# Attention and a mixture of experts on one core: weight copies and K/V loads in two requests, and another sum for the weights' power of two

## The chip, the core and the metric

The kernel runs on one NeuronCore of a Trainium2 chip. Five engines work side by side, each through its own instructions in order: TensorE (PE, matmuls; PEld is its weight load), VectorE (DVE), ScalarE (ACT), GpSimd (POOL) and SyncE (SP), which here asks for most of the transfers. They wait for each other by semaphores. The metric is the device time of one execution in microseconds; lower is better. The program moves data by 16 DMA engines; SP's requests stand in one queue.

## The reference

Four batches of 12288 queries attend to pooled keys; each row of the result goes through one of 8 experts.

```python
kv_pool = kv.reshape(B, H // r, r, W // r, r, C).mean(axis=(2, 4))    # r = 4: 768 keys per batch
k = v = kv_pool.reshape(B, -1, C) @ w_sr                              # C = 128
a = softmax(q @ k.T / sqrt(C));  x = a @ v                            # 4 x 12288 rows
expert = argmax(normalised x . normalised expert_emb / tau)           # 8 experts, gate = its probability
out[rows of e] = gate * (relu(x @ w1[e]) @ w2[e])                     # w1: 128 x 1024, w2: 1024 x 128
```

## The kernel before

Float32 factors are split into two float16 parts, hi and lo, and a product is three matmuls (hi hi, hi lo, lo hi) where that pays. So that no part over- or underflows, a tensor is first divided by a power of two near its largest entry.

The attention runs in 96 steps of 512 queries (`step_ops`), 24 to a batch. A step forms scores in blocks of 128 queries by 768 keys (`s_mm`), takes the row maximum on DVE (`s_max`; from step 16 on `s_leave`, which also moves the scores out of PSUM), the exponential on ACT (`s_exp`), the hi and lo parts (`p_hi`, `p_lo`), turns them by DMA transposes that SP asks for (`p_t`: tiles `pthi`, `ptlo`) and multiplies by V (`av`: `xp`). Until step 16 three PSUM banks of scores take turns, so a score block must wait until the exponential of three blocks before has read its bank. Rows are scattered to DRAM by expert (POOL), and tiles of 256 rows of one expert come back (`load`) and go through `l1` (x times W1), `h_hi` and `h_lo` (the relu's parts, ACT and DVE), `l2` and `l2_lo` (times W2), and a scatter to the output. Attention steps and expert tiles run at the same time from about 220 us on; the expert tiles alone make up the end.

In the first 180 us `w_ops` prepares the experts' weights: loads W1 and W2 (`wf`), takes the largest entry per partition (`w_max`, or a norm by ACT), finds the power of two over all partitions (`pow2_ops`), makes hi and lo parts (`w_hi`, `w_lo`) and stores them in DRAM as rows of `w_prep`. The order in `pow2_ops`, one link after another: a TensorE transpose of the partitions' maxima into `w_m` (line 441), four DVE instructions on `w_t` (maximum, floor, exponent mask, a diagonal: lines 641 to 653), a matmul with ones that spreads the result to all partitions (line 658), a multiply and a reciprocal on DVE (664, 668). K and V use the same function and keep it.

An expert tile `t` needs its expert's row block of `w_prep` in one of three buffers `wbuf` (`load_w`, 1 MB). The request is conditional: where the buffer already holds that expert, the copy is skipped, but SP still works through the request. K and V source rows of the next batch are loaded ahead in 8 pieces (`kv_load`, 768 KB each, line 453), and summed on DVE or POOL (`kv_adds`, line 467).

No order is written by hand. `Plan` collects operations with an engine, a duration, a key (a due time) and the operations they need, plays them through, and records them in the order in which each engine takes them; ready operations go by their key. A table `X` of numbers sets keys and choices of engine. So a change of a duration, a key or a part moves instructions on all engines, far behind its own place. SP's queue is planned with a number for each transfer's length (`dma=`).

Of the kernel before, what the change touches and what calls it, by code (L numbers as in the profile page):

```python
# [11 lines left out]
F16 = mybir.dt.float16  # L12
# [32 lines left out]
X = dict(  # L45
    ka=16, da=8.159, di=14.892, db=12.933, dma=1.729, ahead=2.284, av=6.502, av0=1.846, lb=-4.518, l2=3.102, qt=1.955,
    lead=18.786, x=-14.465, r=0.691, s=-1.205, p=14.572, x0=3.032, r0=2.092, s0=1.377, p0=5.813, qt0=-0.263,
    pm="acabacbccabcccabbdacccb", pl="aaaaabaa", nm="AAADA", xn="DAAA", nm0="ADD", xn0="AA", we="ddcdcdaaadcdaccd",
    h=13.707, kv=20.916, kvs=2.272, w0=-14.405, start=23.312, early=21.36, wd=12.952, xw=1.718, qd=21, qs=21.178,
    ql=9.747, em="---------AA-A-A-A-AA-DM-", et=2.859, ec=-0.864, v0=123.118, sd=1, qu=1.461, q0=-66.525, avd=0.626,  # L50
    m=1.052, end=-3.563, ne=-4.766, ge=-0.689, kd="DPD", gk=547.052, wq="AADADDAD", kv1=10.617, kvs1=0.757, tg=-0.003,
    tl=0.397, qe="------------------------", gap=1.8, nb="ADDDD-DAAD-A---DDD-A--D-----DDD--A-D-A-D-DA----D",
    sqm="AASAAAAAAAAAPAAAPSSAPPPS", qm="AAADDDADDAADDADAAADAAAAD", xh="ADPPDADPDAADDAAPAADADADD", nl="-",
    slack={'ACT PE': 0.131, 'ACT DVE': 0.095, 'ACT POOL': -0.009, 'ACT ACT': -0.082, 'DVE PE': 0.32, 'DVE ACT': 0.274, 'DVE POOL': 0.348, 'DVE DVE': 0.013, 'PE ACT': 0.263, 'PE DVE': 0.071, 'PE POOL': -0.1, 'PE SP': -0.11, 'POOL ACT': 0.46015762370487345, 'POOL DVE': 0.111, 'POOL PE': 0.1, 'POOL POOL': 0.07},
    wt=4.0, leadr=22.0, wr=55.0, pd=4.0, kf=16, kc="DA", kk=2.199, su=-1.199, vk=-5.844, om="AAAADADA", og=2.027,
)
# [3 lines left out]
def attention_moe(  # L60
# [44 lines left out]
    PTB = 4  # L105
    PB = 3
    Q2 = 3
    NP = 6
    QB = 2
    NQR = 8  # L110
    WC = 4 * F + 8
    WD = 4 * F + 32
    SCALE = 1.0 / math.sqrt(C)
# [60 lines left out]
    scales = cpool.tile([P, 5], F32, name="scales")  # L174
    for i, v in enumerate((1.0 / 4, 1.0 / 8192, 1.0 / 16, math.log(PSC), 0.0)):
        nc.gpsimd.memset(scales[:, i : i + 1], v)
# [25 lines left out]
    wi_i = cpool.tile([P, NTILE], I32, name="wi_i")  # L202
    cpool.tile([P, 72], F32, name="fill")
    ctx.enter_context(tc.manual_schedule())
# [49 lines left out]
    class Plan:  # L254
# [36 lines left out]
        def run(self, begin):  # L291
# [23 lines left out]
            while any(count):  # L315
# [116 lines left out]
    extra = ExitStack()  # L432
    kvs.tile([P, 16], F32, tag="lead", name="lead")
    xp = extra.enter_context(tc.tile_pool(name="early", bufs=1))
# [14 lines left out]
    def kv_load(b, h):  # L449

        t = kvs.tile([P, WD // 2], F32, tag="kvt", name=f"kvt{b}_{h}", bufs=2)
        t = t[:NI, : R * QC].rearrange("p (r c) -> p r c", r=R)
# [743 lines left out]

    def w_scale(e, inv, s):
        ws[e].update(s=s, inv=inv)

    def w_out(e, i):  # L1200

        wo = xp.tile([P, 2 * F + 8 * i], F16, tag=f"wo{i}", name=f"wo{e}_{i}", bufs=1)
        ws[e]["wo", i] = wo
        if i:
            inv = ws[e]["inv"]
            V.tensor_tensor(
                out=wo[:, 2 * F :].bitcast(F32), in0=inv[:, 0:1].broadcast_to([P, 4]),
                in1=inv[:, 1:2].broadcast_to([P, 4]), op=ALU.mult,
            )
# [8 lines left out]
    def w_hi(e, i):  # L1218
        if i == 0:
            w_out(e, 0)  # L1220
        hi = ws[e]["wo", i][:, 0:F]
        if w_eng(e, i) == " AD":
            nc.scalar.mul(hi, ws[e]["w", i], ws[e]["s"][:, i : i + 1])
        else:
            nc.scalar.copy(out=hi, in_=ws[e]["w", i])

    def w_lo(e, i):
        hi, lo = (ws[e]["wo", i][:, h * F : (h + 1) * F] for h in range(2))
# [10 lines left out]
    def w_store(e, i):  # L1239
        nc.sync.dma_start(out=wprep[e * P : (e + 1) * P, 2 * i * F : WC if i else 2 * F], in_=ws[e]["wo", i])  # L1240

# [362 lines left out]
    def weights(t, a, n):  # L1604
        return wbuf[turn_of(t)][:, a : a + n]
# [48 lines left out]
    def l2_terms(t, u, h, parts):  # L1654
# [4 lines left out]
        for i, (kk, j, o) in enumerate(terms):  # L1659
            f = 2 * F + (u * fu + kk) * P + o  # L1660
# [9 lines left out]
    def o_gate(t):  # L1670
        m = ts[t]["m"][:, :, 0:1]
        V.tensor_scalar(out=m, in0=m, scalar1=weights(t, 4 * F, 2).bitcast(F32), scalar2=None, op0=ALU.mult)

    def o_out(t):
        m = ts[t]["m"]
        nj = size(t) // P
        if gated(t):
# [482 lines left out]
    for t in range(NTILE):  # L2160
# [97 lines left out]
```

## Time and profile before

| | us |
|---|---|
| Device time, median of 3 runs (lowest to highest) | 1948.01 (1947.91 to 1948.92) |
| The profiled execution's own time | 1946.91 |
| Its span, first to last instruction | 1945.2 |
| TensorE busy | 1906.0 |
| DVE busy | 1675.1 |
| ACT busy | 1468.7 |
| POOL busy | 1289.4 |

The trace is of one execution, so its times are compared with its own time; the median stands 1.1 us above that. A busy TensorE isn't TensorE at its peak, since its matmuls are pipelined, and small gaps between them aren't seen as idle. [...]

### The profile page before, as it was taken

What the parts mean: (1) busy time and instruction counts of PE and PEld (TensorE: products, weight loads), DVE (VectorE), ACT (ScalarE), POOL (GpSimd) and SP (SyncE); (2) the same over time, 40 slices, a digit from 0 to 9 for tenths busy, and PEclk for the clock granted to TensorE, in tenths of its full rate; (3) what the DMA queues carried; (4) which work ended last, traced back from release to release, by engine and by line L of the source; (5) the groups of instructions that cost most, each with busy time, mean ns of one, the idle gap of its engine ahead of it and who ended that gap; (6) DMA issues with size and microseconds to landing.
All of it is one profiled execution on the core that took longest, in us unless ns stands there. A gap on an engine that the chain in (4) does not pass through costs nothing. (4 is left out here: it accounts for less than half of the span.)

```text
span 1945.2 us, 63642 instructions
## 1 busy us (share of the span) xinstructions
PE 1906.0 (98%) x23536; PEld 1676.3 (86%) x23536; DVE 1675.1 (86%) x4037; ACT 1468.7 (76%) x3162; POOL 1289.4 (66%) x1857
## 2 busy tenths in 40 slices
PE   6999999999999999999999999999999999999998
PEld 5787788888888888888888888888888888889998
DVE  7899999988989879989989988998888888886655
ACT  4887877877787778877778877878878788775553
POOL 2547587678777777676676675756756766666654
PEclk9999999999999999999999999999999999999999
DMA  7998989889988999878989899887878677664353
GB/s 258 250 267 207 205 174 183 165 156 164 170 182 173 190 205 175 172 165 157 193 168 175 180 214 180 171 157 155 176 132 173 149 153 152 148 126 86 107 131 109
DMA packets 870922, 333.23 MB, mean 171 GB/s; under 512 B 825794, under 2 KB 836171, under 8 KB 868432
## 3 DMA queue, kind: packets, MB, share of 16 engines
q1 hardware_dynamic: 844624, 274.95, 71.4%
q0 software_dynamic: 24640, 53.53, 9.7%
q8 instruction: 186, 3.05, 0.7%
q14 instruction: 128, 1.05, 0.2%
q10 hardware_dynamic: 1344, 0.66, 0.1%
HBM read 271.41 MB, written 63.19 MB: 172 GB/s over the span
## 5 line engine op out<-in xcount | busy, mean ns | idle before, releaser
L1632 ACT ACTIVATE hh<-ph 128x512 f16<-128x512 f32 x754 | 447.6, 595 | 224.4 <-PE ph L1625 181.2
L1637 DVE SCALAR_TENSOR_TENSOR hl<-ph,hh 128x512 f16<-128x512 f32 x754 | 513.6, 684 | 109.6 <-ACT hh L1632 103.7
L1625 PE MATMUL ph<-x,wbuf 128*128 128x256 f16 x4416 | 593.2, 273 | 3.2 <-DMA wbuf<-w_prep 2.5
L207 POOL DMA_INDIRECT xs_rows<-rows,pi x384 | 442.0, 1151 | 176.5 <-issue 37.8
L207 POOL DMA_INDIRECT out_dram<-o,m x350 | 382.4, 1093 | 229.0 <-ACT o L1681 45.8
L1625 PEld LDWEIGHTS <-wbuf 128*128 128x128 f16 x4848 | 438.9, 98 | 67.4 <-DMA wbuf<-w_prep 2.9
L1661 PE MATMUL po<-wbuf,hh 128*128 128x128 f16 x6032 | 459.9, 219 | 2.9 <-DVE hl L1637 1.1
L1661 PEld LDWEIGHTS <-hh 128*128 128x128 f16 x6176 | 400.0, 98 | 20.6 <-issue 3.8
L810 PE MATMUL s<-k,qT 128*128 128x512 f16 (+1 forms) x1920 | 364.9, 326 | 1.4 <-DVE nm L821 1.4
L821 DVE CUSTOM_DVE_ANT_0 p<-s,scales,qa 128x768 f32<-128x768 f32 x320 | 323.4, 1011 | 41.6 <-PE s L810 38.9
L875 DVE SCALAR_TENSOR_TENSOR plo<-p,phi 128x768 f16<-128x768 f32 x358 | 350.3, 980 | 5.6 <-ACT phi L861 2.4
L840 ACT ACTIVATE p<-p,nm 128x768 f32<-128x768 f32 x320 | 299.0, 934 | 58.8 <-DVE nm L821 56.8
L926 PE MATMUL xp<-v,pthi 128*128 128x136 f16 (+1 forms) x4392 | 319.7, 223 | 1.4 <-ACT q L738 0.8
L1661 PE MATMUL po<-wbuf,hl 128*128 128x128 f16 x3016 | 291.6, 219 | 0.0
L926 PEld LDWEIGHTS <-pthi 128*128 128x128 f16 x4392 | 278.7, 98 | 14.4 <-issue 2.3
L861 ACT ACTIVATE phi<-p 128x768 f16<-128x768 f32 x310 | 260.9, 844 | 5.9 <-DMA pthi<-phi 2.8
L810 PEld LDWEIGHTS <-qT 128*128 128x128 f16 x1920 | 178.6, 98 | 87.4 <-issue 2.3
L1661 PEld LDWEIGHTS <-hl 128*128 128x128 f16 x3088 | 205.1, 98 | 0.6
L926 PE MATMUL xp<-v,ptlo 128*128 128x136 f16 x2196 | 189.8, 223 | 4.3 <-DMA ptlo<-plo 4.3
L946 ACT ACTIVATE x<-xp,rn 128x135 f32<-128x135 f32 x304 | 96.5, 372 | 76.3 <-DVE rn L938 58.2
L960 POOL TENSOR_TENSOR rows<-x,rows 128x256 f16<-128x256 f32 x192 | 137.2, 719 | 18.2 <-ACT rows L956 13.3
L926 PEld LDWEIGHTS <-ptlo 128*128 128x128 f16 x2196 | 144.0, 98 | 4.8 <-DMA ptlo<-plo 4.8
(416 smaller groups left out, 2043.0 us busy)
## 6 DMA issues: line engine op xcount, KB each, us to landing
wbuf<-w_prep SPq DMA_DIRECT2D x202, 1026.0 KB
q<-in_q_dram SPq DMA_DIRECT2D x48, 512.0 KB
kvt<-in_kv_dram SPq DMA_DIRECT2D x24, 768.0 KB
wf<-in_moe_w_dram SPq DMA_DIRECT2D x16, 512.0 KB
kvt<-in_kv_dram SPq DMA_DIRECT2D x12, 512.0 KB
xs_rows<-rows,pi POOLq DMA_INDIRECT x384
out_dram<-o,m POOLq DMA_INDIRECT x350
w_prep<-wo SPq DMA_DIRECT2D x8, 514.0 KB
```

The lines of the kernel that those rows point to most:

```text
L207: ins = nc.gpsimd.indirect_dma_start(out=dst, out_offset=bass.IndirectOffsetOnAxis(ap=idx, axis=0), in_=src, in_offset=None, bounds_check= ...
L810: nc.tensor.matmul(t[:, lo:hi], qs[:, l, :], r[:, lo:hi], start=i == 0, stop=i == 2)
L821: V.tensor_tensor_reduce(out=p, in0=ks[k].pop(("s", j)), in1=scales[:, 4:5].broadcast_to([P, NK]), scale=ks[k]["fac"], scalar=3.0e38, op0= ...
L840: nc.scalar.activation(out=p, in_=s, func=AF.Exp, bias=ks[k].pop(("nm", j)), scale=1.0 if unscaled(k) else -1.0)
L861: nc.scalar.mul(hi, p, PSC)
L875: V.scalar_tensor_tensor(out=lo, in0=ks[k].pop(("p", j)), scalar=PSC, in1=hi, op0=ALU.mult, op1=ALU.subtract)
L926: nc.tensor.matmul(ks[k]["xp", h][:, i, :e], l[:, c, :], r[:, c, :e], start=n == 0, stop=n == len(terms) - 1, skip_group_check=True,)
L960: nc.gpsimd.tensor_tensor(out=r[:, :, C : 2 * C], in0=ks[k]["x"][:, 2 * h : 2 * h + 2, 0:C], in1=r[:, :, 0:C], op=ALU.subtract)
L1625: nc.tensor.matmul(ph[:, kk * n : (kk + 1) * n], weights(t, o + f, P), r, start=i == 0, stop=i == 2)
L1632: nc.scalar.activation(out=hh, in_=ts[t]["ph", u], func=AF.Relu)
L1637: V.scalar_tensor_tensor(out=hl, in0=ts[t].pop(("ph", u)), scalar=0.0, in1=ts[t]["hh", u], op0=ALU.max, op1=ALU.subtract)
L1661: nc.tensor.matmul(ts[t]["po"][:, j * C : (j + 1) * C], h[:, kk * n + j * P : kk * n + (j + 1) * P], weights(t, f, P), start=u == 0 and i ...
```

## The change

Three parts.

First, weight copies of tiles below 176 and all K/V source loads are asked for in two requests. The first half of a weight copy holds W1 and the scale, which moves from the row's end to its middle and is padded to 32 columns (`WS`); the second half holds W2. `l1` waits for the first, `l2` for the second also. The two halves of a K/V load are two of its four rows each; the sums wait for both. The new function `second` puts the other half on SP's queue at the highest priority, 1.5 us by the plan after the first was taken, so that a request that stands ready in between is taken between them.

Second, the weights' power of two comes from the sum over partitions of the partitions' maxima: one matmul with ones (`total`), a floor and factor in one DVE instruction, the exponent mask and the reciprocal. The factor becomes 1/512 where it was 1/4, since a sum over 128 partitions is up to 128 times the maximum. `sum_ops` takes the place of `pow2_ops` in `w_ops`.

Third, numbers in `X` change: due times and offsets of the first 16 steps, the engines of five weight halves' work (`we`), the engine of the first copy of K for batch 0 (`kc`: from DVE to ACT), and the due times of the weights' work.

```diff
-    pm="acabacbccabcccabbdacccb", pl="aaaaabaa", nm="AAADA", xn="DAAA", nm0="ADD", xn0="AA", we="ddcdcdaaadcdaccd",
+    qt0=0.723, pm="acabacbccabcccabbdacccb", pl="aaaaabaa", nm="AAADA", xn="DAAA", nm0="DDD", xn0="AA",
+    we="ddcccdacddadcccd", h=13.707, kv=20.916, kvs=2.272, w0=-13.574, start=23.312, early=21.36, wd=12.917,
...
-                    if op.dma is not None and u.dma is not None and eng == u.eng and not op.lands:
+                    if op.dma is not None and u.dma is not None and eng == u.eng and not op.lands or u.eng == "~t":
                         ready = op.end
...
+        kv_part(b, h, 0)
+
+    def kv_part(b, h, i):
+        r = slice(i * (R // 2), (i + 1) * (R // 2))
         nc.sync.dma_start(
-            out=t, in_=kv[b].rearrange("(i r) w c -> i r (w c)", r=R)[:, :, h * QC : (h + 1) * QC]
-        )
-        st[b]["kvt", h] = t
+            out=st[b]["kvt", h][:, r, :],
+            in_=kv[b].rearrange("(i r) w c -> i r (w c)", r=R)[:, r, h * QC : (h + 1) * QC],
+        )
...
+    def sum_ops(key, e, room, *deps):
...
+        def total():
+            h["pm"] = one_tile(f"w{e}_m")
+            nc.tensor.matmul(h["pm"][:, 0:2], ones2, ws[e]["m"], start=True, stop=True)
+
+        def scaled():
+            h["inv"] = sm.tile([P, 2], F32, tag="pw2w", name=f"w{e}_2")
+            V.scalar_tensor_tensor(
+                out=h["inv"], in0=h["pm"][:, 0:2], scalar=1e-30, in1=scales[:, 0:2], op0=ALU.max, op1=ALU.mult
+            )
...
+        o = first = add("PE", 0.1, key, total, *deps, take=f"w{e}_m")
+        o = add("DVE", 0.2, key, scaled, o, *room, free=f"w{e}_m")
+        o = add("DVE", 0.17, key, power, o)
+        return first, add("DVE", 0.2, key, inverse, o)
...
-        nc.sync.dma_start(out=wbuf[turn_of(t)][:, :WC], in_=wprep[ds(row, P), :], cond=w < E * P)
+        if t >= NA - PER:
+            nc.sync.dma_start(out=wbuf[turn_of(t)], in_=wprep[ds(row, P), :], cond=w < E * P)
+            return
+        ts[t]["w"] = w, row
+        w_part(t, 0)
+
+    def w_part(t, i):
+        w, row = ts[t]["w"]
+        c = slice(2 * F + WS, WD) if i else slice(0, 2 * F + WS)
+        nc.sync.dma_start(out=wbuf[turn_of(t)][:, c], in_=wprep[ds(row, P), c], cond=w < E * P)
...
+    def second(o, key, fn):
+
+        return add("SP", 0.0, -1e6, fn, add("~t", HALF, key, lambda: None, o))
...
             o = took("kvt", add("SP", 0.45, t0, lambda h=h: kv_load(b, h), *turn("kvt", 2), dma=2.6, hold=True))
+            rest = second(o, t0, lambda h=h: kv_part(b, h, 1))
...
-                r = add(ENG[on], KV_ADD[on][i], t0 + 8.0 + 0.1 * i, fn, o, r, *deps, port=True)
+                r = add(ENG[on], KV_ADD[on][i], t0 + 8.0 + 0.1 * i, fn, o, r, rest, *deps, port=True)
...
-            o, sc = pow2_ops(
-                t0 + 1.2 * d, f"w{e}_", lambda e=e: ws[e]["m"], scales[:, 0:2],
-                lambda inv, s, e=e: w_scale(e, inv, s), scaled.get(e - 2, ()), *m,
-            )
+            o, sc = sum_ops(t0 + 1.2 * d, e, scaled.get(e - 2, ()), *m)
...
+        lw2 = second(lw, kw, lambda t=t: w_part(t, 1)) if t < NA - PER else lw
+        o1, o2, ol = None if whole else o1, lw2, None
```

Two places show how the order moves. The first is TensorE's order near the weights of expert 1, in steps 1 and 2. `s_` are the three score banks, `qT1` and `qT2` the queries of steps 1 and 2, `w1_m` the scale of expert 1; the number at a name's end is the buffer's. Before:

```order
L441 MATMUL w1_m_433<-ident_64,wm1_382 2x128
L803 MATMUL s_1_159<-kf0_255,qT1_314 128x512
L803 MATMUL s_1_159<-kf0_255,qT1_314 128x256
L658 MATMUL w1_m_433<-w1_t_442,ones2_95 128x2
L803 MATMUL s_2_160<-kf0_255,qT2_398 128x512
L803 MATMUL s_2_160<-kf0_255,qT2_398 128x256
L441 MATMUL pq3_483<-ident_64,q2_312 128x128 x4
L803 MATMUL s_0_158<-kf0_255,qT2_398 128x512
L803 MATMUL s_0_158<-kf0_255,qT2_398 128x256
```

The same stretch of TensorE's order now:

```order
L837 MATMUL s_1_159<-kf0_255,qT1_312 128x512
L837 MATMUL s_1_159<-kf0_255,qT1_312 128x256
L443 MATMUL pq3_437<-ident_64,q2_316 128x128 x4
L837 MATMUL s_2_160<-kf0_255,qT2_418 128x512
L837 MATMUL s_2_160<-kf0_255,qT2_418 128x256
L695 MATMUL w1_m_477<-wm1_405,ones2_95 128x2
L837 MATMUL s_0_158<-kf0_255,qT2_418 128x512
L837 MATMUL s_0_158<-kf0_255,qT2_418 128x256
```

The two `w1_m` matmuls around the last block of step 1 have become one, which stands behind the first block of step 2, and `pq3`, the turn of step 3's queries, has moved ahead of that block.

The second place is SP's queue where the weights of tile 98 (`wbuf2`) are asked for. `ptlo63_1` is a part of step 63's second half, `x_101` and `m101` are the rows of tile 101, `kvt3_6` is a K/V load; the quiet rows load and check registers. Before:

```order
L904 DMA_TRANSPOSE pthi63_1_25327<-phi63_1_25070 128x12x128
L904 DMA_TRANSPOSE ptlo63_1_25373<-plo63_1_25292 128x12x128
L1554 TENSOR_LOAD off_i_132
L1554 ISA x2
L1592 ISA
L1592 DMA_TRANSPOSE x_101_25422<-xs_rows 128x2x256
L1593 ISA
L1593 DMA m101_25421<-xs_rows 128x2x2
L1554 TENSOR_LOAD wi_i_133
L1554 ISA x2
L1568 ISA
L1568 DMA wbuf2_2878<-w_prep 128x4104
```

SP's queue at the same place now:

```order
L459 DMA kvt3_6_25340<-in_kv_dram 96x2x512
L938 DMA_TRANSPOSE pthi63_1_25472<-phi63_1_25117 128x12x128
L1585 TENSOR_LOAD wi_i_133
L1585 ISA x2
L1608 ISA
L1608 DMA wbuf2_2885<-w_prep 128x2080
L938 DMA_TRANSPOSE ptlo63_1_25535<-plo63_1_25196 128x12x128
L1608 ISA
L1608 DMA wbuf2_2885<-w_prep 128x2048
```

The copy for tile 98 was asked for behind `ptlo63_1` and the loads of tile 101; its first half now stands ahead of `ptlo63_1`, its second half behind it, and the second half of a K/V load stands ahead of `pthi63_1`.

## Rows read from the trace of the kernel before

**Rows 1.** The page, busy us (share of the span) and instructions of each engine.
```profile
PE 1906.0 (98%) x23536; PEld 1676.3 (86%) x23536; DVE 1675.1 (86%) x4037; ACT 1468.7 (76%) x3162; POOL 1289.4 (66%) x1857
```
**Rows 2.** TensorE's waits, whole span: who waited for whom, total, times, longest.
```profile
PE xp L926 <- DMA ptlo<-plo: 4.3, 2, 2.3
PE w_m L658 <- DVE w_t L653: 3.7, 1, 3.7
PE ph L1625 <- DMA wbuf<-w_prep: 2.5, 2, 2.1
...
PE w_m L441 <- DVE rn L937: 0.9, 1, 0.9
...
PE w_m L658 <- DVE rn L937: 0.5, 1, 0.5
```
**Rows 3.** Timeline of TensorE from 45 us: start, us, operation, idle before and releaser.
```profile
45.43 0.58 PE L658 MATMUL w_m<-w_t,ones 2*128 2x2 f32 x2 [3.67 <-DVE w_t L653]
45.94 2.93 PE L803 MATMUL s<-kf,qT 128*128 128x512 f32 x4
...
49.21 1.46 PE L803 MATMUL s<-kf,qT 128*128 128x512 f32 x4
```
**Rows 4.** Windows: length; PE, PEld, DVE, ACT, POOL busy; PEclk; DMA share; GB/s.
```profile
40.00:45.00 5.00, 1.59 (x5) 0.68 (x4) 5.00 (x11) 5.00 (x7) 1.77 (x1) 1.00 0.53 119
...
46.00:47.00 1.00, 1.00 (x3) 0.48 (x3) 0.97 (x4) 1.00 (x2) 1.00 (x1) 0.50 1.73 166
...
712.00:716.00 4.00, 4.00 (x46) 3.31 (x45) 2.72 (x8) 3.52 (x10) 2.17 (x4) 1.00 0.67 158
...
1165.00:1170.00 5.00, 5.00 (x45) 3.71 (x43) 2.28 (x4) 2.36 (x4) 2.53 (x4) 0.66 0.75 133
```
**Rows 5.** Timeline of DVE, first and fourth link of expert 1's scale.
```profile
41.25 0.27 DVE L641 TENSOR_REDUCE w_t<-w_m 2x1 f32<-2x128 f32 x1
...
43.89 1.48 DVE L653 TENSOR_SCALAR w_t<-ident,w_t 2x2 f32<-2x2 f32 x1
```
**Rows 6.** Timeline of ACT, the exponential that frees the next score bank.
```profile
44.00 0.89 ACT L840 ACTIVATE p<-s,nm 128x768 f32<-128x768 f32 x1
```
**Rows 7.** Timeline of TensorE, both old matmuls of a scale and their followers.
```profile
64.87 0.27 PE L441 MATMUL w_m<-ident,wm 128*2 128x128 f32 x1
64.98 1.46 PE L803 MATMUL s<-kf,qT 128*128 128x512 f32 x4
...
84.56 0.38 PE L658 MATMUL w_m<-w_t,ones 2*128 2x2 f32 x2
84.87 0.87 PE L441 MATMUL s<-ident,p 128*128 128x128 f32 x6
```
**Rows 8.** Timeline of TensorE, two waits for transfers.
```profile
708.74 0.53 PE L926 MATMUL xp<-v,ptlo 128*128 128x136 f16 x6 [2.29 <-DMA ptlo<-plo]
...
1163.98 0.83 PE L1625 MATMUL ph<-x,wbuf 128*128 128x256 f16 x6 [2.13 <-DMA wbuf<-w_prep]
```
**Rows 9.** Weight copy requests (ns min/median/max), and timeline of SP's queue.
```profile
L1568 SPq DMA_DIRECT2D wbuf<-w_prep x202: 73/88/384, 216.9 to 1928.8; - x101
...
695.27 3.10 SPq L904 DMA_TRANSPOSE pthi<-phi  x1
698.48 5.26 SPq L790 DMA_TRANSPOSE qT<-q  x1
...
1151.98 1.34 SPq L904 DMA_TRANSPOSE ptlo<-plo  x1
...
1157.61 0.35 SPq L1568 DMA_DIRECT2D wbuf<-w_prep  x1
```
**Rows 10.** Waits of DVE and POOL for K/V loads, 100 to 1300 us.
```profile
DVE kvt L467 <- DMA kvt<-in_kv_dram: 0.9, 2, 0.7
...
POOL kvt L467 <- DMA kvt<-in_kv_dram: 6.3, 3, 2.8
```
**Rows 11.** Windows, columns as in rows 4.
```profile
1200.00:1400.00 200.00, 200.00 (x2535) 177.02 (x2533) 179.36 (x438) 160.43 (x352) 135.44 (x209) 1.00 0.82 163
```

More of the change, by code (lines that the diff above doesn't have):

```diff
@@ L45 @@
 X = dict(
-    ka=16, da=8.159, di=14.892, db=12.933, dma=1.729, ahead=2.284, av=6.502, av0=1.846, lb=-4.518, l2=3.102, qt=1.955,
-    lead=18.786, x=-14.465, r=0.691, s=-1.205, p=14.572, x0=3.032, r0=2.092, s0=1.377, p0=5.813, qt0=-0.263,
-    pm="acabacbccabcccabbdacccb", pl="aaaaabaa", nm="AAADA", xn="DAAA", nm0="ADD", xn0="AA", we="ddcdcdaaadcdaccd",
-    h=13.707, kv=20.916, kvs=2.272, w0=-14.405, start=23.312, early=21.36, wd=12.952, xw=1.718, qd=21, qs=21.178,
-    ql=9.747, em="---------AA-A-A-A-AA-DM-", et=2.859, ec=-0.864, v0=123.118, sd=1, qu=1.461, q0=-66.525, avd=0.626,
@@ L51 @@
[L51 to L54, printed above, removed]
@@ L55 @@
-    wt=4.0, leadr=22.0, wr=55.0, pd=4.0, kf=16, kc="DA", kk=2.199, su=-1.199, vk=-5.844, om="AAAADADA", og=2.027,
+    ka=16, da=8.159, di=14.892, db=12.933, dma=1.729, ahead=2.284, av=6.502, av0=2.087, lb=-4.518, l2=3.102,
+    qt=1.955, lead=18.786, x=-14.465, r=0.691, s=-1.205, p=14.572, x0=3.203, r0=1.391, s0=0.724, p0=3.241,
+    qt0=0.723, pm="acabacbccabcccabbdacccb", pl="aaaaabaa", nm="AAADA", xn="DAAA", nm0="DDD", xn0="AA",
+    we="ddcccdacddadcccd", h=13.707, kv=20.916, kvs=2.272, w0=-13.574, start=23.312, early=21.36, wd=12.917,
@@ new lines @@
+    xw=1.718, qd=21, qs=21.178, ql=9.747, em="---------AA-A-A-A-AA-DM-", et=2.12, ec=-5.592, v0=114.919, sd=1,
+    qu=1.461, q0=-51.038, avd=0.626, m=1.052, end=-3.563, ne=-4.766, ge=-0.689, kd="DPD", gk=549.765,
+    wq="AADADDAD", kv1=10.617, kvs1=0.757, tg=-0.003, tl=0.397, qe="------------------------", gap=1.8,
+    nb="ADDDD-DAAD-A---DDD-A--D-----DDD--A-D-A-D-DA----D", sqm="AASAAAAAAAAAPAAAPSSAPPPS",
+    qm="AAADDDADDAADDADAAADAAAAD", xh="ADPPDADPDAADDAAPAADADADD", nl="-",
+    slack={'ACT PE': 0.131, 'ACT DVE': 0.095, 'ACT POOL': -0.009, 'ACT ACT': -0.082, 'DVE PE': 0.32, 'DVE ACT': 0.274, 'DVE POOL': 0.348, 'DVE DVE': 0.013, 'PE ACT': 0.263, 'PE DVE': 0.071, 'PE POOL': -0.1, 'PE SP': -0.11, 'POOL ACT': 0.46, 'POOL DVE': 0.111, 'POOL PE': 0.1, 'POOL POOL': 0.07},
@@ L56 @@
+    wt=4.0, leadr=22.0, wr=55.0, pd=4.0, kf=16, kc="AA", kk=0.921, su=-0.362, vk=-4.62, om="AAAADADA", og=2.027,
 )
@@ L106, in attention_moe @@
     PB = 3
+    HALF = 1.5
     Q2 = 3
@@ L110, in attention_moe @@
     NQR = 8
-    WC = 4 * F + 8
-    WD = 4 * F + 32
+    WS = 32
+    WD = 4 * F + WS
     SCALE = 1.0 / math.sqrt(C)
@@ L174, in attention_moe @@
     scales = cpool.tile([P, 5], F32, name="scales")
-    for i, v in enumerate((1.0 / 4, 1.0 / 8192, 1.0 / 16, math.log(PSC), 0.0)):
+    for i, v in enumerate((1.0 / 512, 1.0 / 8192, 1.0 / 16, math.log(PSC), 0.0)):
         nc.gpsimd.memset(scales[:, i : i + 1], v)
@@ L202, in attention_moe @@
     wi_i = cpool.tile([P, NTILE], I32, name="wi_i")
-    cpool.tile([P, 72], F32, name="fill")
+    cpool.tile([P, 8], F32, name="fill")
     ctx.enter_context(tc.manual_schedule())
@@ L432, in attention_moe @@
     extra = ExitStack()
-    kvs.tile([P, 16], F32, tag="lead", name="lead")
+    kvs.tile([P, 32], F32, tag="lead", name="lead")
     xp = extra.enter_context(tc.tile_pool(name="early", bufs=1))
@@ L451, in kv_load @@
         t = kvs.tile([P, WD // 2], F32, tag="kvt", name=f"kvt{b}_{h}", bufs=2)
-        t = t[:NI, : R * QC].rearrange("p (r c) -> p r c", r=R)
+        st[b]["kvt", h] = t[:NI, : R * QC].rearrange("p (r c) -> p r c", r=R)
+        kv_part(b, h, 0)
+    def kv_part(b, h, i):
+        r = slice(i * (R // 2), (i + 1) * (R // 2))
         nc.sync.dma_start(
-            out=t, in_=kv[b].rearrange("(i r) w c -> i r (w c)", r=R)[:, :, h * QC : (h + 1) * QC]
+            out=st[b]["kvt", h][:, r, :],
+            in_=kv[b].rearrange("(i r) w c -> i r (w c)", r=R)[:, r, h * QC : (h + 1) * QC],
         )
-        st[b]["kvt", h] = t
     def kv_pooled(b, h):
@@ L680, in pow2_ops, with power, inverse @@
         o = add("DVE", 0.2, key, scaled, o, *room, free=f"{name}m")
+        return first, add("DVE", 0.2, key, inverse, o)
+    def sum_ops(key, e, room, *deps):
+        h = {}
+        def total():
[6 more added lines that the diff above has]
+            )
+        def power():
+            i = h["inv"].bitcast(I32)
+            V.tensor_scalar(out=i, in0=i, scalar1=0x7F800000, scalar2=None, op0=ALU.bitwise_and)
+        def inverse():
+            s = sm.tile([P, 2], F32, tag="pw3w", name=f"w{e}_3")
+            V.reciprocal(out=s, in_=h["inv"])
+            ws[e].update(s=s, inv=h["inv"])
+        o = first = add("PE", 0.1, key, total, *deps, take=f"w{e}_m")
+        o = add("DVE", 0.2, key, scaled, o, *room, free=f"w{e}_m")
+        o = add("DVE", 0.17, key, power, o)
         return first, add("DVE", 0.2, key, inverse, o)
@@ L1195, in w_norm @@
         V.tensor_scalar(out=m, in0=m, scalar1=float(64 << 23), scalar2=None, op0=ALU.add)
-    def w_scale(e, inv, s):
-        ws[e].update(s=s, inv=inv)
     def w_out(e, i):
-        wo = xp.tile([P, 2 * F + 8 * i], F16, tag=f"wo{i}", name=f"wo{e}_{i}", bufs=1)
+        wo = xp.tile([P, 2 * F + WS * i], F16, tag=f"wo{i}", name=f"wo{e}_{i}", bufs=1)
         ws[e]["wo", i] = wo
@@ L1206, in w_out @@
             V.tensor_tensor(
-                out=wo[:, 2 * F :].bitcast(F32), in0=inv[:, 0:1].broadcast_to([P, 4]),
-                in1=inv[:, 1:2].broadcast_to([P, 4]), op=ALU.mult,
+                out=wo[:, 0:WS].bitcast(F32), in0=inv[:, 0:1].broadcast_to([P, WS // 2]),
+                in1=inv[:, 1:2].broadcast_to([P, WS // 2]), op=ALU.mult,
             )
@@ L1220, in w_hi @@
             w_out(e, 0)
-        hi = ws[e]["wo", i][:, 0:F]
+        hi = ws[e]["wo", i][:, WS * i : WS * i + F]
         if w_eng(e, i) == " AD":
@@ L1227, in w_lo @@
     def w_lo(e, i):
-        hi, lo = (ws[e]["wo", i][:, h * F : (h + 1) * F] for h in range(2))
+        hi, lo = (ws[e]["wo", i][:, WS * i + h * F : WS * i + (h + 1) * F] for h in range(2))
         if w_eng(e, i) == " AD":
@@ L1239, in w_store @@
     def w_store(e, i):
-        nc.sync.dma_start(out=wprep[e * P : (e + 1) * P, 2 * i * F : WC if i else 2 * F], in_=ws[e]["wo", i])
+        nc.sync.dma_start(out=wprep[e * P : (e + 1) * P, 2 * i * F : WD if i else 2 * F], in_=ws[e]["wo", i])
     def setup(key, *deps):
@@ L1671, in o_gate @@
         m = ts[t]["m"][:, :, 0:1]
-        V.tensor_scalar(out=m, in0=m, scalar1=weights(t, 4 * F, 2).bitcast(F32), scalar2=None, op0=ALU.mult)
+        V.tensor_scalar(out=m, in0=m, scalar1=weights(t, 2 * F, 2).bitcast(F32), scalar2=None, op0=ALU.mult)
     def o_out(t):
@@ L1685, in o_out @@
             out=o, in0=ts[t].pop("po").rearrange("p (j c) -> p j c", c=C),
-            scalar=weights(t, 4 * F, 2).bitcast(F32), in1=m[:, :, 0:1].broadcast_to([P, nj, C]),
+            scalar=weights(t, 2 * F, 2).bitcast(F32), in1=m[:, :, 0:1].broadcast_to([P, nj, C]),
             op0=ALU.mult, op1=ALU.mult,
```

5 lines of the change are left out of this document (2 added, 3 removed).

## The prediction

> **What bounds the kernel now.** I read the page's busy table first. TensorE is busy 1906.0 us of a 1945.2 us span, and no other engine passes 86% [rows 1]. The two matmul stages and the attention share one instruction stream on TensorE, so whatever makes that stream wait is added to the end. The chain of waits is of no use here (it holds one output scatter at the very end), so I went to TensorE's own waits. Ahead of its first matmul it waits for the start-up, which stays. [Rows 2] has the waits that the change can reach: 3.7 us for the weights' scale chain (`w_m` from `w_t`), 0.9 and 0.5 us on the same `w_m` matmuls for other DVE work, 4.3 us for two `ptlo` transposes, and 2.5 us for the expert weights `wbuf`.
>
> The rows at each place then give the price of a wait, which is more than its length. At 45.43 us the wait is 3.67 us, and the score block behind it takes 2.93 us, where the next one takes 1.46 [rows 3]. [...] The wait for `wbuf` at 1163.98 us is 2.13 us, and then the clock's mean is 0.66 from 1165 to 1170 us, which costs another 0.34 x 5 = 1.7 us. After the 2.29 us wait at 708.74 us the clock stayed at 1.00 from 712 to 716 us [rows 4, 8]; a wait of about 2 us may or may not lower it.
>
> **A. The weights' power of two.** For each of 8 experts the old chain is a TensorE transpose, four small DVE instructions, a TensorE spread, a multiply and a reciprocal. The new one is one matmul with ones, then three DVE instructions. The old chain is slow because its links stand between long DVE instructions: for expert 1 the first link starts at 41.25 us and the fourth at 43.89 us, where it took 1.48 us itself [rows 5], and TensorE, in order, waited for all of it.
>
> *A1, the wait at 45.43.* Its whole price is the 3.67 us, 2.93 - 1.46 of the block behind it, and 0.58 - 0.38 of the slowed `w_m` [rows 3, 7]: 5.3 us. What is late next is ACT: the score block of step 2 needs a bank that the exponential `p1_1` frees, and that exponential ran from 44.00 to 44.89 us [rows 6]. In the new order ACT has nearly the same work ahead of it, and on TensorE `pq3` is already done and `w1_m` comes behind the block. So the block starts at about 44.9. At full speed the block after it then starts at 44.9 + 1.4 + 0.3 = 46.6 instead of 49.21, 2.6 us sooner. If TensorE's wait for ACT still lowers the clock, it is 44.9 + 2.9 + 0.6 = 48.4, 0.8 us sooner. If ACT is early, up to 5.3. I take 2.6, since the wait shrinks to about 2.5 us, near the one at 708.74.
>
> *A2.* The 0.5 us on the second `w_m` matmul go with that instruction. The 0.9 us belong to the first one, which needs the same maxima as before. I take 0.5, between 0 and 1.4.
>
> *A3, TensorE's own work.* The transpose moves the next instruction by 0.11 us (64.87 to 64.98), the spread by 0.31 (84.56 to 84.87) [rows 7]. The new matmul with ones is not in the trace with these operands; its nearest rows are those two, so it costs between 0.11 and 0.31. I take 0.31, its nearer neighbour by shape: 8 x 0.11 = 0.9 us saved (up to 8 x 0.31 = 2.5). The 24 DVE instructions saved, and the two weight halves that move from DVE to POOL, are off TensorE's path once A1 is counted: nothing more.
>
> **B. Halves of the weight copies.** Most requests are skipped, since the buffer holds the right expert: the median request is 88 ns, while one that copies takes SP about 0.35 [rows 9]. Of the 176 requests that are now split only nine have that length before 1700 us, three when a new expert begins, three times; the last of them is the one at 1157.61. The other second requests cost SP some 0.1 us each; SP waits for other engines far longer, so I put them at 0.
>
> *B1, the wait at 1163.98.* The copy was requested at 1157.61 [rows 9] and landed 6.4 us later, behind two transposes. Now its first half (W1 and the scale) stands three requests further up, ahead of `ptlo63_1`, whose old request was at 1151.98 [rows 9], and only W1 is needed for the first matmul. That is 4 us or more earlier where 2.13 are needed: 3.8 us with the clock. If `ptlo63_1` makes SP wait, less; bounds 0 to 3.8.
>
> *B2, the wait at 708.74.* A copy and a K/V load had just been asked for; `pthi` then took SP 3.10 us and `qT` 5.26 us, where 1.3 is usual, so the queue was full and `ptlo` was asked for only behind both [rows 9]. In the new order the copies for tiles 49 and 50 are spread between transposes and the second is cut in two, but both halves of the K/V load still precede `ptlo39_1`. I take half of 2.3, 1.2 us; bounds 0 and 2.3.
>
> *B3, the other 2.0 us on `ptlo`* (4.3 - 2.3) follow a K/V load, too. There the new order has load half, `pthi`, load half, `qT`, `ptlo`: everything that was ahead of `ptlo` still is. I take 0, between 0 and 2.0.
>
> **C. Halves of the K/V loads.** All 24 load requests become two with about one transpose between, so the sums of rows that need both halves start later by about 1.5 to 2 us. Now DVE waited 0.9 us in 2 of 16 loads, POOL 6.3 us in 3 of 8 [rows 10]. Behind a waiting sum on DVE stand the score maxima and `hl` that TensorE needs. I take a loss of 1.5 us (two or three DVE waits, a third of them reaching TensorE); bounds 0 and 10.7. The upper end: each of 16 loads makes DVE wait 2 us, 32 us, and a third reaches TensorE, since DVE is 90% busy (179.36 of 200 us) [rows 11] and has little slack.
>
> [...]
>
> **The sum.** 2.6 + 0.5 + 0.9 + 3.8 + 1.2 + 0 - 1.5 = 7.5 us saved. The profiled execution took 1946.91 us (span 1945.2 and 1.7 outside it), so 1939.4; the median of the runs shown, 1948.01, is 1.1 above it, so 1940.5 us. The change also re-plans everything behind step 16; the small waits that this redraws (0.2 to 1.4 us each) I count as equal before and after.
>
> **Rivals.**
> 1. *The waits change hands.* TensorE waits for `p` from ACT where it waited for `w_t`, the clock falls there, the copies are awaited in another place: A1 0.8, A3 0.9, the rest nothing: 1948.0 - 1.7 = 1946.3 us. For it: ACT is full from 40 to 45 us, and `p1_1` is next in line. Against it: the copy at 1164 moves up by more than its wait. This counts as no change.
> 2. *The K/V sums wait on DVE.* Price 10.7 us, with A's 4.0 saved and B's gain lost: 1948.0 + 10.7 - 4.0 = 1954.7 us, slower. It decides if DVE's waits for `kvt` between 100 and 1300 us rise from 0.9 us to over 25. For it: the sum now depends on a request that SP issues behind a transpose, which can take 5 us when the queue is full. Against it: the plan keys the sums 8 us behind the request, and 14 of 16 did not wait.
> 3. *Nearly all reachable waits go*, with the clock: 5.3 + 1.4 + 0.9 + 3.8 + 2.3 + 2.0 = 15.7 us, 1932.3 us.
>
> **The numbers.** Forecast 0.54 (own range 1934 to 1944), rival 3 0.10, rival 1 0.21, rival 2 0.15. A measurement of this kernel tells about 0.2%, 3.9 us, from no change: faster means under 1944.1, slower over 1951.9. So faster 0.64, same 0.21, slower 0.15. The range 1932 to 1949.5 takes in rival 3's end and rival 1, and leaves most of rival 2 out.
>
> **What would show it.** A1: no wait for `w_t`, a wait for `p` of under 3 us near 42 to 45 us, and the granted clock at 1.00 there. B1: no wait of `ph` for `wbuf` after 1100 us and no low clock behind it. B2: the `ptlo` wait near 700 us under 1.5 us. C: DVE's waits for `kvt` under 5 us. I am wrong if TensorE's busy time, not its waits, changes by more than 3 us, or if new waits over 1.5 us appear in the stretch after 225 us that these terms do not name.

## The result and the profile after

The changed kernel takes 1962.12 us (median of 6 runs, 1958.38 to 1965.70), the kernel before, run beside it, 1947.95 (6 runs): ratio 1.0085, 95% interval 1.0069 to 1.0102. So it is slower, by 14 us; 1940.5 was forecast, and 1932 to 1949.5 was the range. The profiled execution took 1960.03 us, its span 1958.0.

TensorE's work is what it was [rows 1]. First the busy line of the page, then TensorE's waits in the changed kernel (who waited for whom, total, times, longest), and the stretch that answers to rows 3:

```profile
PE 1907.6 (97%) x23528; PEld 1677.5 (86%) x23528; DVE 1672.0 (85%) x4012; ACT 1470.9 (75%) x3163; POOL 1290.1 (66%) x1859
```
```profile
PE s L837 <- ACT p L874: 6.4, 5, 2.5
PE ph L1665 <- ACT x L980: 4.4, 3, 2.8
PE po L1701 <- DVE hl L1677: 3.9, 5, 1.4
...
PE ph L1665 <- DMA wbuf<-w_prep: 0.4, 1, 0.4
```
```profile
45.15 2.93 PE L837 MATMUL s<-kf,qT 128*128 128x512 f32 x4 [2.54 <-ACT p L874]
...
48.11 1.54 PE L837 MATMUL s<-kf,qT 128*128 128x512 f32 x4
```

The waits that the change was to reach are gone: `w_t`, both for `ptlo`, and 0.4 is left of 2.5 for `wbuf` [rows 2]. The wait for `p` at 45.15 us is 2.54, as foreseen, but the granted clock (PEclk in the windows, a share of full speed) is 0.50 from 45 to 48 us, so the block behind it takes 2.93 us and the next one starts at 48.11, only 1.1 us sooner than before [rows 3]. TensorE's busy time differs by 1.6 us; its idle time (span less busy) rises from 39.2 to 50.4 us. So most of the loss is new waits elsewhere.

To see where, I count matmuls. This table says how much later a kernel has issued as many matmuls as the kernel before at that time (us, worked out from the number of matmuls in windows of 5 us of one execution each, good to about 1 us as to the counting; other runs stand beside it, they are told of below):

```
before's time     100   160   200   300   500   700   800  1000  1200  1300  1850
changed          -1.7  -5.6   3.7   6.5   6.5  11.3   8.4   9.7  12.9  14.2  12.6
e14 (all parts,
 order kept)     -0.5  -1.0  -2.3   0.8   3.6   4.9   6.1   7.8  15.1  19.3  19.2
e13 (weight
 halves, kept)   -0.6   0.0   2.7   2.8   5.5   8.8  14.9  15.2  22.5  22.8  21.3
e17 (requests
 alone, kept)    -0.4  -0.8  -0.5  -0.6   0.8   6.3   7.9   7.6   9.1   9.4  10.1
e18 (changed,
 copies whole)   -0.8  -5.4   3.7   4.7   5.0   7.5   3.8   3.5   7.4   7.3   6.3
e15 (changed,
 K/V whole)      -1.6  -5.6   3.9   5.6   7.7  12.6   8.8  10.8  19.7  20.8  19.5
```

The changed kernel is 5.6 us ahead at 160 us. By 200 us all of that and 3.7 us more is lost, and the rest goes in small steps until 1300 us. The windows of that stretch (columns as in rows 4), the changed kernel first, then the kernel before:

```profile
160.00:200.00 40.00, 34.25 (x219) 25.52 (x218) 37.78 (x97) 30.16 (x73) 23.32 (x28) 0.91 0.68 161
...
185.00:186.00 1.00, 0.48 (x2) 0.00 (x0) 0.97 (x5) 1.00 (x3) 0.75 (x1) 0.50 0.00 0
```
```profile
160.00:200.00 40.00, 38.73 (x291) 30.72 (x290) 38.29 (x108) 33.99 (x80) 27.90 (x30) 1.00 0.76 182
```

TensorE was busy 34.25 of 40 us where it had been 38.73. Behind the first of these two waits the granted clock fell (0.80 from 184 to 185 us, then 0.50); it was low already before the second, and stayed so until 191 us:

```profile
183.55 1.93 PE L837 MATMUL s<-kf,qT 128*128 128x512 f32 x4 [2.28 <-ACT p L874]
...
186.53 1.11 PE L443 MATMUL pq<-ident,q 128*128 128x128 f32 x4 [1.05 <-ACT x L980]
```

The sums of the K/V source wait more, as rival 2 had it, but less than its 25 us (DVE, 100 to 1300 us; 0.9 before [rows 10]):

```profile
DVE kvt L473 <- DMA kvt<-in_kv_dram: 14.6, 7, 3.2
```

### The profile page after: what moved, and what is told of

Same layout as the page of the kernel before. It is cut to its first block, busy times and chain, and to the rows that moved or that the text cites. A ratio compares the mean times of both kernels' runs of the same rounds, so it can differ in the third digit from the quotient of the medians.

```text
span 1958.0 us, 64252 instructions
## 1 busy us (share of the span) xinstructions
PE 1907.6 (97%) x23528; PEld 1677.5 (86%) x23528; DVE 1672.0 (85%) x4012; ACT 1470.9 (75%) x3163; POOL 1290.1 (66%) x1859
## 5 line engine op out<-in xcount | busy, mean ns | idle before, releaser
L209 POOL DMA_INDIRECT xs_rows<-rows,pi x384 | 436.0, 1135 | 178.7 <-issue 40.6
L209 POOL DMA_INDIRECT out_dram<-o,m x350 | 373.5, 1067 | 242.5 <-ACT o L1721 43.8
```

Of the source, the lines that this page charges most:

```text
L209: ins = nc.gpsimd.indirect_dma_start(out=dst, out_offset=bass.IndirectOffsetOnAxis(ap=idx, axis=0), in_=src, in_offset=None, bounds_check= ...
```

## The experiments

The kernels were timed in five sets (e1 to e4, e5 to e8, e9 to e12, e13 to e16, e17 and e18), each beside the kernel before. Its median was 2002.58, 2003.74, 2014.20, 1944.57 and 1945.42 us in them, so every number below is a ratio to the kernel before in the same set; brackets are 95% intervals. The first three sets differ from the other two in more than time: in the traces of e1 to e12 TensorE stands idle 39 to 66 times, 15 to 34 us in all, for nothing that the profile shows, and in those of before, the changed kernel and e13 to e18 never. Why is not known. So a ratio of the first three sets and one of the last two, set side by side, show more than the edit.

The theories: T1, the K/V sums are planned for a landing that the second half misses; T2, the new numbers crowd VectorE from 160 to 190 us; T3, any new plan loses, because the numbers had been fitted to the old one; T4, the halves cost by themselves. Two came later: T5, the places of tiles in SBUF decide; T6, a request costs SP's queue time even when it is skipped.

**Parts alone, with the old numbers (e1 to e4).**

```diff
 e1: -whole K/V load              +kv_part(b, h, 0); second(o, t0, kv_part(b, h, 1))
 e2: -whole weight copy           +w_part(t, 0); second(lw, kw, w_part(t, 1))
 e3: -o, sc = pow2_ops(...)       +o, sc = sum_ops(...)
 e4: the changed kernel with the table X of before
```


> Only the K/V loads are split; whole weight copies, the old power of two and the old numbers. Theory 1 (the sums of K/V rows are planned for a landing that the second half misses, DVE stands still and TensorE behind it): DVE waits for kvt of 10 us or more between 100 and 1300 us, time 5 to 9 us above before. Theory 2 (the new numbers of the first 16 steps crowd DVE from 160 to 190 us): DVE waits for kvt may rise, time within 3 us of before. Theory 3 (any re-planning of the order moves the time, no part by itself): 0 to 6 us either way, not tied to the kvt waits.

> Only the weight copies are split; whole K/V loads, the old power of two and the old numbers. Theory 1: the waits for wbuf at 1164 us go with their low clock, 2 to 5 us below before. Theory 2: the same, since neither K/V nor the numbers are touched. Theory 3: up to 6 us either way.

> Only the weights' power of two is worked out by the sum; whole transfers and the old numbers. Theory 1 and 2: the wait at 45 us and its low clock shrink, 2 to 5 us below before. Theory 3: up to 6 us either way; a loss of over 3 us speaks for it.

> Sum and both splits as in the changed kernel, with the old table of numbers. Theory 1: DVE waits for kvt of 10 us or more stay, time 0 to 6 us above before. Theory 2: the loss of the changed kernel from 160 to 190 us is gone, time 3 to 8 us below before. Theory 3: anything within 10 us of before.

Measured: e1 1.0026 [1.0006, 1.0045], e2 1.0061 [1.0032, 1.0090], e3 1.0052 [1.0031, 1.0072], e4 1.0073 [1.0045, 1.0100]. Every part alone is slower. This seemed to speak for T3. But in the traces of e1 and e2 TensorE, VectorE, ScalarE and GpSimd have the instructions of before in the order of before (the plan gives the second halves no length; eight small VectorE instructions write a wider scale); only in e3 and e4 does the order change. So e1 and e2 can't be cases of T3. T2 expected the loss from 160 to 190 us to be gone in e4. It is not: with the old numbers TensorE is busy 33.46 of 40 us from 160 to 200 us (33.47 in e3), by other waits than in the changed kernel. So a loss there doesn't need the new numbers.

**The order of before kept (e5 to e7), and a new order alone (e8).** In e5 to e7 the plan is before's, and the changed instructions are put where the old ones stood, a second half at the first request planned 1.5 us behind the first.

```diff
 e5:  w_part(t, 0); half(w_part(t, 1))     # fill: 72 -> 56 columns, for room
 e6:  kv_part(b, h, 0); half(kv_part(b, h, 1))
 e7:  turn -> matmul with ones; top, floor, power, diagonal, spread -> nothing
 e8: -da=8.159   +da=8.162
```


> The kernel before with its plan left as it was, so that TensorE, VectorE, ScalarE and GpSimd get their instructions in the order of before; only the weight copies go as two halves, the second at the first request of SP that is planned 1.5 us or more behind the first. Two theories of the order: T3 (a new plan loses, the halves don't) expects the loss of the same edit under a new plan (1.0061) to be gone: ratio 0.998 to 1.001, with TensorE's waits for wbuf and ptlo (6.8 us in before) down to 0 to 3 us. T4 (the halves lose by themselves: more requests on SP, transposes and loads later) expects 1.003 to 1.007 again. T1 (sums of the K/V source too early) and T2 (new numbers of the first 16 steps) have nothing here and expect 0.998 to 1.001.

> The kernel before with its plan left as it was; only the K/V source loads of batches 1 to 3 go as two halves, the second at the first request of SP planned 1.5 us or more behind the first. T1 expects the sums of the source, which stand where they stood, to wait for the second half: VectorE's waits for kvt from 0.9 us to 10 us or more, and 1.002 to 1.004 by the waits of TensorE behind them. T3 expects 0.999 to 1.001, since no instruction changes its place. T4 expects 1.002 to 1.004 by later transposes, without waits for kvt.

> The kernel before with its plan left as it was; only the chain of the weights' power of two is the short one: the matmul with ones where the transpose stood, nothing where the maximum, floor, power, diagonal and the second matmul stood, the three new VectorE instructions where the scaling and the reciprocal stood. VectorE has 24 instructions less. T3 expects 0.998 to 1.000 (in place of 1.0052 under a new plan), at best the 3.7 us wait for w_t gone. A theory that the sum itself costs (T4) expects 1.003 or more again. T1 and T2 expect 0.998 to 1.000.

> The kernel before with one number of its table changed by 0.04% (the length of one of the first 16 steps, 8.159 to 8.162) and nothing else: the same instructions, planned anew, and VectorE has about 2,500 of 4,012 in the same sequence. T3 expects a loss as large as those of the parts: 1.002 to 1.007. T1, T2 and T4 know nothing that this could cost: 0.999 to 1.001.

Measured: e5 1.0383 [1.0360, 1.0405], e6 1.0027 [1.0013, 1.0040], e7 1.0009 [0.9993, 1.0025], e8 1.0073 [1.0053, 1.0094]. The sum is free where the order stays, and costs 0.5% where the plan is drawn anew (e3); one number 0.04% off costs 0.7% with no other change. T3 holds for these. K/V halves cost 0.3% without any new plan, against T3; VectorE's waits for `kvt` are 2.7 us in e6, so not by the 10 us of T1 either. And e5 was a surprise: its instructions are e2's, in the same order on all five engines; only addresses in SBUF differ. By the programs, `q`, `p`, `pthi`, `ptlo` and `qT` start at multiples of 256 bytes in e2 and in before, and 64 bytes below one in e5 (its `fill` is 16 columns of 4 bytes narrower).

**Places in SBUF (e9 to e11), and the changed kernel beside them (e12).**

```diff
 e9:  e5 with fill of 40 columns (places of before modulo 128 bytes)
 e10: e5, e6 and e7 together, fill 40
 e11: before with  -cpool.tile([P, 72], F32, name="fill")  +cpool.tile([P, 56], F32, name="fill")
 e12: the changed kernel
```


> The edit of the run with the weight copies halved under the kept order (1.0383), with a filling tile of 40 in place of 56 columns, so that every large SBUF tile starts at the same remainder of 128 bytes as in before; order and requests are the same, word for word. T5 (the place of tiles in SBUF decides there: q, p, pthi, ptlo and qT stood 64 bytes off) expects 1.000 to 1.006 in place of 1.0383. T4 (the halves lose by themselves) expects 1.0383 again, if it was the halves that made it, or 1.004 to 1.006 if that run was made by the places and 1.0061 of the weight halves alone by the halves. T3 (only a new plan loses) expects 0.998 to 1.001: nothing but SP's requests is moved.

> All three parts of the change in the order that before's plan gives to TensorE, VectorE, ScalarE and GpSimd, with before's remainders of 128 bytes for the large tiles. T3 expects 0.997 to 1.001, since no engine is planned anew. T4 expects the sum of the parts under the kept order: 1.003 (K/V halves) and 0 to 0.006 (weight halves) and 0.001 (sum), 1.003 to 1.009. T1 expects 1.002 to 1.004 by VectorE's waits for kvt.

> The kernel before with the filling tile 56 in place of 72 columns wide: all tiles behind it stand 64 bytes lower in SBUF, and no instruction is changed or moved. T5 expects 1.02 to 1.04, with the share of the DMA queue q1 up from 1390 us of 16 engines' time to about 1480 us, and ScalarE waiting tens of us for q. Without T5: 0.999 to 1.001.

> The changed kernel itself, beside the others of this call. Its ratio elsewhere was 1.0085 (1.0069 to 1.0102); every theory expects 1.006 to 1.011 here. If it is under 1.004, what it loses depends on more than the kernel, and the ratios of the parts can't be added up to it.

Measured: e9 1.0360 [1.0331, 1.0388], e10 1.0338 [1.0302, 1.0374], e11 1.0182 [1.0155, 1.0208], e12 1.0062 [1.0039, 1.0086]. Moving the tiles by 64 bytes costs 1.8% with no instruction changed. The page's line of SP's DMA queue (packets, MB, share of 16 engines' span) of e11, of e12 in the same set, and of the kernel before:

```profile
q1 hardware_dynamic: 844624, 274.95, 73.5%
```
```profile
q1 hardware_dynamic: 846304, 275.11, 68.7%
```
```profile
q1 hardware_dynamic: 844624, 274.95, 71.4%
```

That is 0.735 x 2040.9 = 1500 us of transfer in e11. The same packets and bytes take 0.714 x 1945.2 = 1389 us in the kernel before (its trace is of another set), and the changed kernel's nearly equal ones 0.687 x 2022.2 = 1389 in e12. My guess of the remainder was too small: by the programs, all kernels that were not slow agree with before modulo 256 bytes in these tiles, e9 and e10 only modulo 128. So e5, e9 and e10 don't answer what they were made for.

**At the right places (e13, e14), K/V loads whole (e15), another number (e16).**

```diff
 e13: e5 with fill of 8 columns (places modulo 256)
 e14: e10 with fill of 8 columns
 e15: the changed kernel, -kv_part(...)/second(...)  +whole K/V load
 e16: -ahead=2.284   +ahead=2.285
```


> The weight copies in two halves, order of the four engines as in before, and a filling tile of 8 columns, so that the large SBUF tiles start at before's remainders of 256 bytes (the run before kept only those of 128). T5 (places modulo 256) expects 1.000 to 1.007 in place of 1.036. T3 (only a new plan costs) expects 0.998 to 1.001, T4 (the halves cost by themselves) 1.004 to 1.008. If it is 1.03 again, the places are not what made the two runs slow.

> All three parts in before's order of the four engines, with before's remainders of 256 bytes for the large tiles. T3 expects 0.997 to 1.002, so that the whole loss of the changed kernel (1.0062 to 1.0085) is its new plan. T4 expects the sum of the parts, 1.006 to 1.010: then the new plan and numbers of the changed kernel give nothing back.

> The changed kernel with its K/V source loads in one piece; the order of the four engines is the changed kernel's, and SP has 24 requests less. T1 expects VectorE's waits for kvt back from 14.6 to 1 to 3 us and the ratio down by 0.002 to 0.004, to 1.003 to 1.005. T3 expects it unchanged, 1.006 to 1.0085, since the plan is the same. T4 expects 1.003 to 1.006.

> The kernel before with another number of its table changed by 0.04% (how far ahead SP's requests are planned, 2.284 to 2.285): the same instructions planned anew, VectorE with 2,864 of 4,012 in the same sequence. T3 expects 1.002 to 1.008 as for the other number (1.0073). T4, T1 and T5 expect 0.999 to 1.001.

Measured: e13 1.0115 [1.0096, 1.0135], e14 1.0109 [1.0088, 1.0129], e15 1.0103 [1.0085, 1.0120], e16 1.0037 [1.0023, 1.0051]. So most of the 3.6% is gone with the remainder of 256, though e13 stays above T5's range (1.000 to 1.007), and it was timed in another set than e5 and e9. What speaks for T5 without that doubt is e11 in its own set, and e5 against e2 (1.0383 and 1.0061, the same instructions, kernel before at 2003.74 and 2002.58). Which of the tiles it is was not tried. T4 holds and is larger than I thought: halves of the weight copies cost 1.15% with every engine's order as before and the places as before modulo 256, and all parts together cost no more. T1 falls: with whole K/V loads VectorE's waits for `kvt` from 100 to 1300 us are 4.8 us in place of 14.6, and the time is no better than the changed kernel's. e16 confirms T3 at half the size.

In the first 200 us e14 answers for T2's place: 160 to 200 us with the changed kernel's parts in before's order, and at 45 us, where the sum replaced the wait for `w_t`.

```profile
160.00:200.00 40.00, 38.73 (x301) 31.05 (x300) 38.48 (x109) 34.54 (x80) 26.92 (x31) 1.00 0.73 172
```
```profile
45.48 2.11 PE L862 MATMUL s<-kf,qT 128*128 128x512 f32 x4 [3.20 <-ACT p L899]
```

From 160 to 200 us TensorE is busy 38.73 us as in before, at a granted clock of 1.00; in e15 and e18, which have the changed kernel's order but whole K/V loads or whole copies, it is busy 34.19 and 33.30. So it is the changed kernel's order there that loses, not its parts. The 2.28 us wait for `p` there goes back to a row maximum of VectorE at 181.61 us, for which ScalarE waited 2.43 us and which stands behind small instructions of tile selection; VectorE as a whole is no fuller (37.78 us busy, 38.29 before). That is read from the trace only; it wasn't tried by itself. And at 45 us the sum under the old order only hands the wait over: 3.67 us for `w_t` have become 3.20 for `p`.

Where does e13 lose? Under the old order the halves don't bring what they were made for. TensorE's waits for `wbuf` rise from 2.5 us to 5.4 in e13, and in e18 (below), whose copies are whole but whose order is the changed kernel's, they fall:

```profile
PE ph L1649 <- DMA wbuf<-w_prep: 5.4, 2, 2.7
```
```profile
PE ph L1665 <- DMA wbuf<-w_prep: 1.3, 1, 1.3
```

What is left in e18 stands at 1826.7 us; the wait at 1164 us is gone there without halves, and stays in e13 with them (2.6 us at 1173.7).

ScalarE waits too, for the queries' loads. These are its waits for `q` before, in e13, in e17 (below) and in e14:

```profile
ACT qjunk L710 <- DMA q<-in_q_dram: 18.2, 11, 4.3
```
```profile
ACT qjunk L724 <- DMA q<-in_q_dram: 35.9, 18, 5.0
```
```profile
ACT qjunk L724 <- DMA q<-in_q_dram: 23.3, 13, 4.3
```
```profile
ACT qjunk L769 <- DMA q<-in_q_dram: 18.8, 11, 5.6
```

But e14 loses as much as e13 with ScalarE's waits for `q` as before, so these waits are not the whole of it, and the way from later requests to TensorE is not shown.

What every second request costs, SP shows. A step of its queue before (start, us it takes, request), and in e13 with a skipped second half in it:

```profile
443.97 0.40 SPq L1593 DMA_DIRECT2D m<-xs_rows  x1
444.47 2.14 SPq L904 DMA_TRANSPOSE pthi<-phi  x1
```
```profile
448.00 0.40 SPq L1617 DMA_DIRECT2D m<-xs_rows  x1
448.80 0.07 SPq L1592 DMA_DIRECT2D wbuf<-w_prep  x1
448.98 1.43 SPq L918 DMA_TRANSPOSE pthi<-phi  x1
```

From the end of `m` to `pthi` is 0.10 us before and 0.58 in e13: the skipped request is seen for 0.07 us but takes 0.48 out of the queue. The rest of that gap is SP's register work for it (0.21 us), the wait on a semaphore and small gaps. There are 176 of them, some 84 us of SP's time at that price, where I had counted 0.1 us each and then nothing.

**The requests alone (e17), and the copies whole again (e18).**

```diff
 e17: +half(lambda: nc.sync.dma_start(out=fill[:, 0:8].bitcast(F16),
      +     in_=wprep[ds(row, P), 0:16], cond=w > E * P + 4094))   # never holds
 e18: the changed kernel, -w_part(t, 0); second(...)  +whole copy
```


> The kernel before, copies and loads whole, with 176 more requests on SP: at each place where the halves had their second one, a conditional request of 4 KB whose condition never holds, so that it moves nothing. Theory T6 (a request costs SP's queue about 0.5 us even when skipped: 0.59 us between two transposes with a skipped second half between them, 0.10 without; transposes and q loads behind it are later) expects most of the 1.0115 of the weight halves: 1.006 to 1.012, with ScalarE's waits for q up from 18 us to 30 us or more. The rival (two pieces with others between land later or disturb the transposes) expects 0.999 to 1.002.

> The changed kernel with its weight copies in one piece again; the order of the four engines is the changed kernel's and its K/V loads and sum stay. T4 and T6 (the halves of the weight copies cost, by their requests) expect 0.996 to 1.001, the loss of the changed kernel gone. T3 (a new plan costs) expects 1.004 to 1.009, since the plan is the changed kernel's.

Measured: e17 1.0065 [1.0041, 1.0090], e18 1.0058 [1.0041, 1.0076]. In e17 SP's requests are before's, in the same order, with 176 skipped ones between them. At the 105 places where the neighbours stood less than 0.2 us apart before, the median gap goes from 0.10 to 0.52 us, so the 0.48 us of that one place are typical (0.42).

Requests that move nothing cost about half of what the halves cost (1.0065 against 1.0115), so T6 holds for that half; ScalarE's waits for `q` rise less than expected (23.3 us, not 30). The rest is with the pieces themselves or with what runs between them, which no run separates. In the traces SP's requests use eight landing semaphores in turn (in before 1154 of 1163 requests have that of the one eight places ahead), and a request waits on the one it uses (1149 of 1171 do), so more requests may hold the queue for that reason too; this wasn't tried. e18 falls in T3's range: T4 and T6 are wrong that the changed kernel's loss goes with the halves. In the table e18 goes with the changed kernel until 200 us, the loss of the new order from 160 to 200 us included. From 200 to 1300 us it loses another 3.6 us where the changed kernel loses 10.5, which would be the halves' part. It is not clear of noise: the changed kernel itself measured 1.0062 in e12, its six runs beside the first result spread over 7 us, and e15, with the halves and another trace, loses 16.9 there.

## Why the prediction was wrong

The waits went as foreseen: none for `w_t`, `p` awaited 2.54 us at 45.15 (foreseen under 3), 0.4 us for `wbuf`, none for `ptlo`. But what they were worth, and what removed them, did not.

A1, 2.6 us, was mis-sized. It took the clock to stay up behind a wait of about 2.5 us, as at 708.74 us, and counted on 1.00 there; it was 0.50 from 45 to 48 us, and had been 0.50 from 46 to 47 before [rows 4], and the next block came 1.1 us sooner. This is near rival 1's price for A1 (0.8), and e14 has its mechanism: the wait changes hands. All of A was put at 4.0 us. The changed kernel leads by 5.6 us at 160 us, but e14, with the sum under the old order, by 1.0: most of that lead is the new order's.

B1 and B2 have the right numbers, but the halves did not earn them. The wait for `wbuf` at 1164 us went with the earlier request, which B1 named and which is the new order's: it is gone in e18, whose whole copy is asked for at 1152.63 us (1157.61 before), and not in e13 with halves. The `ptlo` wait near 700 us stays with the halves under the old order (2.2 us in e13) and with the new order and whole copies (2.1 in e18); it is gone only where the new order and both kinds of halves come together. That the queue was full near 700 us before is my reading of the 3.10 and 5.26 us that two requests took [rows 9]; what held them is not shown.

Two steps failed that turn the sign.

*"The other second requests cost SP some 0.1 us each; SP waits for other engines far longer, so I put them at 0."* A skipped request takes 0.4 to 0.5 us of SP. Measured alone, under the kept order, the 176 of them cost 0.65% (12.7 us), and the halves of the weight copies in all 1.15%. So SP's waits for other engines (721 us in all before) did not absorb them; that its slack is an average, and often absent ahead of a query load or a turn, is my reading and is not shown. In the changed kernel, whose order is another, taking the halves out gives back about 5 us by the traces (spans 1958.0 and 1952.9), which the ratios don't set clear of noise (1.0085 and 1.0062 against 1.0058).

*"the small waits that this redraws (0.2 to 1.4 us each) I count as equal before and after."* They are not. A plan drawn anew cost 0.4% and 0.7% where a single number moved by 0.04%, and 0.5% for the sum, which costs nothing (1.0009) under the old order. The changed kernel's new order loses about 9 us between 160 and 200 us, with whole K/V loads (e15) and whole copies (e18) too, and the same parts under the old order don't lose it. All three orders drawn anew without the halves (e3, e8, e16) are slower than before's, so before's order is a good one among those near it; I priced the instructions and took the order as neutral.

C, the K/V halves, I put at 1.5 us: under the old order they cost 0.26 and 0.27%, some 5 us (e1 and e6, one order on all five engines). In the changed kernel whole loads gave nothing back. Rival 2 had the right sign and the wrong mechanism: VectorE waited 14.6 us for `kvt`, under its 25. B3's 2.0 us did go, where I took 0. My own sign of error came true in TensorE's 2.84 us wait for `x` of ScalarE at 700.69 us (the longest of the line `ph` from `x` above), which no term names.

Open: how the 0.5% between e17 and e13 arises; why e2 (1.0061) and e13 (1.0115), one order of the same instructions at places that differ in `hh`, `hl` and `o`, measure differently in two sets, of which the first is one of those with TensorE's unexplained idle time; why the new order loses what it loses; and how the loss after 270 us divides between the halves and the order. The changed kernel's order with all transfers whole, which would tell, was not run. No version run here is faster than the kernel before.

## What to carry to other kernels

Where the order of work is fitted to its numbers, price a change twice: the parts under the old order, and a control that only draws the order anew; a gain smaller than the control's loss may not be had without a new fit. Before a wait that has gone is put down to a part, run the new order without that part. Count requests on a queue by the gap that they make between their neighbours, not by their own length, and also those that are skipped (here 0.42 us each, not 0.07). When a tile changes size, keep the places of the others, or an experiment measures the places (here 64 bytes were worth 1.8%).

## What was not expected of the hardware

A shift of 64 bytes in SBUF, with no instruction changed, made the kernel 1.8% slower, and its DMA queue's transfers took 1500 us where those of the kernel before took 1389 in its own trace; with the weight halves 128 bytes off it was 3.6%, against 1.15% and 0.61% at the old remainder of 256 (three sets). A conditional request that is skipped is seen for 0.07 us and costs SP 0.4 to 0.5. And the granted clock fell to 0.50 behind waits of 2.54 us (45 us) and 2.28 us (184 us) in the changed kernel, but stayed at 1.00 behind the one of 2.29 us at 708.74 us before [rows 4, 8].
